# The first slot table of an attention and expert kernel, built by GpSimd instead of VectorE

## The chip, the cores and the metric

The kernel runs on one core of one Trainium2 chip. The metric is the device time of one execution in microseconds (us). Before the change, three runs took 536.79, 538.61 and 538.71 us; their median is 538.61 us. One more execution was recorded by the profiler: 537.63 us, of which its span covers 535.7 us.

The engines are named as in the profile: PE is TensorE (matmuls; PEld its weight loads), DVE is VectorE, ACT is ScalarE, POOL is GpSimd, SP is the engine that issues most transfers. An engine executes its own instructions in the order in which they stand, and waits on semaphores for the others.

## The reference, cut to what matters

Two stages follow each other: attention with rotary positions for 4 batches of 8 heads, 576 tokens and 64 features a head, and then a layer of 8 experts in which each token goes to one expert.

```
scores = scale * matmul(rotate(q), rotate(k).T);  attn = softmax(scores);  x = attn @ v     # x: [4, 576, 512]
logits = x @ w_gate                                                                      # 8 experts
for b in range(B):
    prev_e = -1
    for s in range(S):
        fresh_e = argmax(logits[b, s])
        if s == 0 or local_gate[b, s] < 0.5:  e = fresh_e
        else:                                 e = prev_e if prev_e >= 0 else fresh_e
        prev_e = e
        p = softmax(logits[b, s])
        out[b, s] = p[e] * (maximum(x[b, s] @ w1[e], 0) @ w2[e])
```

The choice of expert depends on the token before, so the tokens of an expert are known only when a batch is through attention. The kernel therefore counts them, gives each token a slot in a tile of 128 tokens of one expert, gathers the tokens of a tile by an indirect transfer, and multiplies tile by tile.

## The kernel before, in words

Attention runs over 16 pairs of heads (index p), each in 9 steps of 128 query rows, 144 steps in all (index g). A step has the score product on PE (line 273, `mm_s`), its minimum on DVE (278, `softmax_min`; the scores are negated, so the minimum is the largest score), the exponential on ACT (295), four transposes on PE (332, `tr_main`), a split of the transposed values into two parts on ACT and DVE (310 and 314, `split_to`), or in five late steps on POOL (305 and 307, `split_by_pool`), and the product with v (371, `pv_mm`), whose result ACT and DVE take out of PSUM (381 and 382).

The first three batches finish before the last one. While the last batch is in attention, their routing is computed in small parts, one a step (`route` and `early`, in the order of the string `ORDER`): logits, the largest, which token starts afresh, the expert (`experts`), and each token's rank among the tokens of its expert (`ranks`). Two results matter here. `ohr` (line 646, written by POOL in 15 comparisons of 128 x 128) holds for each block of 128 tokens a one where a token's rank modulo 128 equals the column. `tcode` (line 648) holds for each token a number made of its expert and the multiple of 128 in its rank.

The function `slots` turns these into lists of tokens. `spread_tokens` compares the codes of the n tiles with `tcode` of the tokens (line 683, a table w of 128 x (nblk x n)), and multiplies the table with the two halves of the tokens' numbers (line 687, `rhs`). `gather_tokens` multiplies `ohr` by `rhs` on PE (line 695, tile `idx`) and makes the row numbers `gidx` (700). `slots` is used twice: with first = 0, for the first six tiles from three batches (nblk = 15, n = 6), in the middle of the last batch's attention; and with first = 6, for the other 19 tiles (nblk = 20).

After the list, POOL issues the indirect transfers of the first tiles (`gather`, line 956; tile `x`). Ahead of them in its order stand the splits of the first two eighths of expert weights (`split_early`, lines 895 and 896). A tile then is transposed (`turn_x`, line 967, tile `tx`), multiplied by w1 (`first_product`, line 981, tile `h`), transposed again (1015) and multiplied by w2 (`second_product`, line 1024, tile `o`).

What sets the order: up to step 126 (g < GM) all engines follow the order of the code. From step 127 on only PE follows it (`MAN0`, later `MAN2` with DVE from the end of attention); the other engines' instructions are put in order by a scheduler when the program is built, from its own costs. The slot table falls in this last stretch, in step 140. On PE it is therefore fixed that the `idx` products (695) follow the value products of pair 14, and that the transposes `tx` of the first tile (letter x in `DRAIN`) follow all value products of pair 15 (letter u), and stand ahead of the last gate products (457) and of `h`.

Of the kernel before, what the change touches and what calls it, by code (L numbers as in the profile page):

```python
# [17 lines left out]
ALU = mybir.AluOpType  # L18
# [119 lines left out]
def tile_attention_moe(ctx, tc, qk, v, tabs, turn, consts, tri, wg, wts, out):  # L138
    nc = tc.nc
    pe, act, dve, pool, sp = nc.tensor, nc.scalar, nc.vector, nc.gpsimd, nc.sync  # L140
# [245 lines left out]
    tcode = const.tile([P, NBLK], F32, name="tcode")  # L386
# [6 lines left out]
    def bc(ap, axis, n):  # L393
        ap = ap.unsqueeze(axis)
        shape = list(ap.shape)
        shape[axis] = n
        return ap.to_broadcast(shape)
# [3 lines left out]
    def small(shape, tag, dt=F32, bufs=1):  # L401
        return sm_p.tile(shape, dt, tag=tag, name=f"{tag}_{next(ctr)}", bufs=bufs)
# [268 lines left out]
    def slots(codes, nblk, first, n):  # L671

        st = {}

        def spread_tokens():
            if first == 0:
                w, rhs = small([P, nblk * n], "c8", BF16), small([P, nblk * n * 2], "ex", BF16)
            else:
                w = et_p.tile([P, S], F32, tag="et", name="slw").bitcast(BF16)[:, 0:nblk * n]
                rhs = et_p.tile([P, S], F32, tag="et", name="slr").bitcast(BF16)[:, 0:nblk * n * 2]  # L680
            w = w.rearrange("p (j n) -> p j n", n=n)
            rhs = rhs.rearrange("p (c j n) -> p c j n", n=n, c=2)
            dve.tensor_tensor(w, bc(codes(), 1, nblk), bc(tcode[:, 0:nblk], 2, n), op=ALU.is_equal)
            yield

            tokp = C["tokp"].rearrange("p (c j) -> p c j", c=2)[:, :, 0:nblk]
            dve.tensor_tensor(rhs, bc(w, 1, 2), bc(tokp, 3, n), op=ALU.mult)
            yield
            st["rhs"] = rhs

        def gather_tokens():
            yield "pe"
            ps = ps_t.tile([P, 2, n], F32, tag="t", name=f"idx_{first}")
            for j in range(nblk):
                pe.matmul(ps, ohr[:, j], st["rhs"][:, :, j], start=(j == 0), stop=(j == nblk - 1))
            yield
            hi = small([P, n], "ihi")
            dve.tensor_scalar(hi, ps[:, 0], 64.0, None, op0=ALU.mult)
            yield
            dve.tensor_tensor(gidx[:, first:first + n], hi, ps[:, 1], op=ALU.add)  # L700
            dve.tensor_tensor(hi, hi, ps[:, 1], op=ALU.add)
            yield
            st["hi"] = hi

        def scatter_tokens():
            hi = st["hi"]
            pad = small([P, n], "ipad")
            dve.tensor_scalar(pad, hi, 0.0, BIG, op0=ALU.is_equal, op1=ALU.mult)
            yield
            dve.scalar_tensor_tensor(sidx[:, first:first + n], pad, -1.0, hi, op0=ALU.add, op1=ALU.add)  # L710
            yield

        return [spread_tokens, gather_tokens, scatter_tokens]

    def tile_experts(inc, first, n):
# [739 lines left out]
```

## Time and profile before

| engine | busy us of 535.7 | share |
|---|---|---|
| PE | 515.3 | 96% |
| DVE | 377.4 | 70% |
| POOL | 346.1 | 65% |
| ACT | 345.3 | 64% |

The profiled execution took 537.63 us, its span is 535.7 us, so 1.93 us lie around the span. An engine's busy share is a mean over stages with different limits: in attention several engines are nearly full at a time, in the expert stage PE is full and the rest have room. The chain of work that ended last runs 80% on PE and 8% on DVE. What a change is worth is read from the stage in which it stands, here from about 270 us to 292 us: the end of attention and the start of the first expert tile.

### The profile page before, as it was taken

How to read it: one execution, taken by the hardware profiler on the slowest of the kernel's cores; microseconds unless marked ns; L12 is line 12 of the kernel's file. 1: busy time of each engine (PE TensorE's matmuls, PEld its weight loads, DVE VectorE, ACT ScalarE, POOL GpSimd, SP SyncE). 2: the span in 40 equal slices, each digit the busy share in tenths (PEclk: the TensorE clock that was granted, in tenths of full speed). 3: DMA queues.
4: the chain of work that ended last, by engine and by line, in shares of the span. 5: the costliest groups of instructions: out<-in, count | busy, mean ns of one | idle time of the engine just before them, and what ended most of it. 6: DMA issues, size and time to landing. Idle time of an engine off the chain costs nothing.

```text
span 535.7 us, 10815 instructions
## 1 busy us (share of the span) xinstructions
PE 515.3 (96%) x3273; PEld 458.9 (86%) x3273; DVE 377.4 (70%) x690; ACT 345.3 (64%) x766; POOL 346.1 (65%) x290
## 2 busy tenths in 40 slices
PE   7989999999999999999999899999999999999992
PEld 4889999999999999998978688887888888888881
DVE  6999999999999999999998746446421745411540
ACT  3988999999999999998877323252533344523440
POOL 4999999999999999983898202255412554411331
PEclk9999999999999999999999999999999999999997
DMA  8658788988879878866167214653446586537440
GB/s 280 275 133 224 224 221 232 236 188 215 221 224 246 200 194 211 239 150 159 24 210 227 65 55 142 190 205 127 169 105 231 150 325 182 181 90 235 107 151 25
DMA packets 65481, 97.33 MB, mean 182 GB/s; under 512 B 28353, under 2 KB 39105, under 8 KB 65282
## 3 DMA queue, kind: packets, MB, share of 16 engines
q1 hardware_dynamic: 61938, 86.45, 57.1%
q0 software_dynamic: 3040, 9.71, 5.6%
q8 instruction: 28, 0.46, 0.4%
q14 instruction: 43, 0.35, 0.3%
q10 hardware_dynamic: 432, 0.36, 0.2%
HBM read 76.95 MB, written 12.86 MB: 168 GB/s over the span
## 4 chain that ended last, share of the span: by engine, by line
PE 80%; DVE 8%; issue 4%; ACT 3%; POOL 2%; DMA 1%; ACTq 0%; POOLq 0%; DVEq 0%
PE h L981 19%; PE o L1024 17%; PE pv L371 14%; PE s L273 13%; PE tm L332 9%; PE gx L457 3%; DVE mn L278 2%; PE th L1015 2%; DVE ptl L314 2%; PE tx L967 2%; ACT e L295 1%; PE tk L342 1%; DMA turn<-in_turn_dram 1%; ACT pth L310 1%; DVE w L926 1%
## 5 line engine op out<-in xcount | busy, mean ns | idle before, releaser
L1024 PE MATMUL o<-w,hs 128*128 128x512 f32 x456 | 113.1, 398 | 0.0
L278 DVE TENSOR_REDUCE mn<-s 128x1 f32<-128x576 f32 x144 | 107.1, 743 | 2.3 <-PE s L273 1.1
L981 PE MATMUL h<-w,xs 128*128 128x512 f32 x444 | 106.4, 393 | 1.3 <-DVE xs L314 1.0
L295 ACT ACTIVATE e<-s,mn 128x576 f32<-128x576 f32 x128 | 95.5, 746 | 15.2 <-DVE mn L278 12.6
L1030 POOL DMA_INDIRECT out_dram<-os,sidx x19 | 23.1, 1213 | 125.4 <-ACTq L932 83.7
L314 DVE TENSOR_TENSOR ptl<-tm,pth 128x512 fp32r<-128x512 f32 x139 | 95.4, 687 | 11.5 <-ACT pth L310 8.8
L273 PE MATMUL s<-m,qst 128*128 128x288 f32 x512 | 96.2, 310 | 4.1 <-ACT e L295 3.0
L981 PEld LDWEIGHTS h<-w,xs 128*128 128x128 f32 x444 | 82.5, 188 | 19.9 <-DVE w L926 1.5
L1024 PEld LDWEIGHTS o<-w,hs 128*128 128x128 f32 x456 | 83.1, 188 | 17.0 <-DVE hs L314 0.4
L310 ACT CAST pth<-tm 128x512 fp32r<-128x512 f32 x139 | 80.7, 581 | 6.8 <-PE tm L332 6.2
L273 PEld LDWEIGHTS s<-m,qst 128*128 128x128 f32 x512 | 74.1, 188 | 9.0 <-ACT e L295 5.1
L371 PE MATMUL pv<-pth,v 128*128 128x288 f32 x256 | 76.8, 315 | 0.6 <-DVE ptl L314 0.4
L332 PE MATMUL tm<-wid,e 128*128 128x128 f32 x512 | 77.1, 272 | 0.0
L371 PE MATMUL pv<-ptl,v 128*128 128x288 f32 x256 | 76.5, 314 | 0.2 <-POOL ptl L307 0.2
L200 POOL TENSOR_TENSOR stage<-stage 128x1152 f32<-128x1152 f32 x26 | 69.4, 2669 | 1.1 <-DMA stage<-in_qk_dram 1.1
L332 PEld LDWEIGHTS tm<-wid,e 128*128 128x128 f32 x512 | 62.1, 140 | 0.8 <-DVE ptl L314 0.4
L926 DVE TENSOR_TENSOR w<-stage,w 128x1024 fp32r<-128x1024 f32 x37 | 51.2, 1418 | 14.6 <-ACT w L923 9.7
L371 PEld LDWEIGHTS pv<-pth,v 128*128 128x128 f32 x256 | 48.3, 189 | 2.0 <-DVE ptl L314 0.7
L371 PEld LDWEIGHTS pv<-ptl,v 128*128 128x128 f32 x256 | 48.3, 189 | 0.5 <-POOL ptl L307 0.4
L314 DVE TENSOR_TENSOR xs<-tx,xs 128x512 fp32r<-128x512 f32 x19 | 13.1, 688 | 44.9 <-ACTq L932 35.0
L201 POOL TENSOR_TENSOR stage<-stage 128x576 f32<-128x576 f32 x26 | 37.1, 1427 | 2.0
L314 DVE TENSOR_TENSOR hs<-th,hs 128x512 fp32r<-128x512 f32 x26 | 17.4, 687 | 28.1 <-ACTq L932 16.6
(202 smaller groups left out, 821.7 us busy)
## 6 DMA issues: line engine op xcount, KB each, us to landing
stage<-in_wts_dram SPq DMA_DIRECT2D x84, 512.0 KB
stage<-in_qk_dram SPq DMA_DIRECT2D x26, 576.0 KB
qst<-xq SPq DMA_DIRECT2D x56, 128.0 KB
stage<-in_v_dram SPq DMA_DIRECT2D x16, 320.0 KB
m<-xq SPq DMA_DIRECT2D x14, 288.0 KB
m<-xk SPq DMA_DIRECT2D x14, 288.0 KB
m<-xq SPq DMA_DIRECT2D x14, 256.0 KB
m<-xk SPq DMA_DIRECT2D x14, 256.0 KB
```

What stands on the lines that cost most here:

```text
L200: engine.tensor_tensor(x, x, tab[:, 2 * f:2 * f + 2], op=ALU.mult)
L201: engine.tensor_tensor(rr[:, f], x[:, 0], x[:, 1], op=ALU.add)
L273: pe.matmul(st[:, h, lo:hi], lhs, keys[:, k0:k0 + hi - lo], start=(n == 0), stop=(n == len(parts_) - 1))
L278: dve.tensor_reduce(mn, s_t[g][:, :, 0:HALF], axis=AX.XY, op=ALU.min)
L295: act.activation(dst.rearrange("p (h s) -> p h s", h=2), s_t.pop(g)[:, :, 0:HALF], AF.Exp, bias=mn, scale=-1.0, accum_out=sums[:, col:col ...
L310: act.copy(hi, src)
L314: dve.tensor_tensor(lo, src, hi.bitcast(F32), op=ALU.subtract)
L332: pe.transpose(ps[:, k], src[:, k * P:(k + 1) * P], ident)
L371: pe.matmul(pv_t[p, u], lhs.rearrange("p c d -> p (c d)"), rhs, start=(n == 0), stop=(n == 9))
L926: (pool if k in on_pool else dve).tensor_tensor(lo, src, hi.bitcast(F32), op=ALU.subtract)
L981: pe.matmul(ps[:, c], xs_t[t][:, x, k], w[y][:, c * 512:(c + 1) * 512], start=(k == 0 and n == 0), stop=(k == 3 and n == 2))
L1024: pe.matmul(ps, hs_t[t][:, x, k], w[y][:, (k % 2) * 512:(k % 2 + 1) * 512], start=(k == 0 and n == 0), stop=(k == 7 and n == 2))
```

## The change

For the first use of `slots` (first = 0) the comparison table is written by POOL, in six instructions, one for each slot (tile) k: each compares 15 token codes a partition with one number, and writes every sixth element of w. The product with the tokens' numbers is given to POOL too. The second use (first = 6) keeps both on DVE. All lines behind line 683 move down by 4.

```diff
@@ -680,11 +680,15 @@
             w = w.rearrange("p (j n) -> p j n", n=n)
             rhs = rhs.rearrange("p (c j n) -> p c j n", n=n, c=2)
-            dve.tensor_tensor(w, bc(codes(), 1, nblk), bc(tcode[:, 0:nblk], 2, n), op=ALU.is_equal)
+            if first == 0:
+                for k in range(n):
+                    pool.tensor_scalar(w[:, :, k], tcode[:, 0:nblk], codes()[:, k:k + 1], None, op0=ALU.is_equal)
+            else:
+                dve.tensor_tensor(w, bc(codes(), 1, nblk), bc(tcode[:, 0:nblk], 2, n), op=ALU.is_equal)
             yield
 
             tokp = C["tokp"].rearrange("p (c j) -> p c j", c=2)[:, :, 0:nblk]
-            dve.tensor_tensor(rhs, bc(w, 1, 2), bc(tokp, 3, n), op=ALU.mult)
+            (pool if first == 0 else dve).tensor_tensor(rhs, bc(w, 1, 2), bc(tokp, 3, n), op=ALU.mult)
             yield
```

On POOL, before, in the last steps of attention (`ptl`, `pth`: split of transposed values; `v`: values of pair 15; `w_m`, `w_q`: the first two eighths of weights; `x`: the gathered tokens):

```order
L219 TENSOR_TENSOR v_15_4354<-stage,v_15_4354 128x10x64
L307 TENSOR_TENSOR ptl_4301<-stage,pth_4300 128x128 x3
L895 TENSOR_SCALAR w_m<-stage 128x1024
L896 TENSOR_TENSOR w_m<-stage,w_m 128x1024
L895 TENSOR_SCALAR w_q_4927<-stage 128x1024
L896 TENSOR_TENSOR w_q_4928<-stage,w_q_4927 128x1024
L956 DMA x_4938<-rows_d,gidx 128x513 x4
```

On POOL, now, at the same place (`c` is the table w, `ex` is rhs):

```order
L219 TENSOR_TENSOR v_15_4354<-stage,v_15_4354 128x10x64
L307 TENSOR_TENSOR ptl_4301<-stage,pth_4300 128x128 x3
L685 TENSOR_SCALAR c_27_4809<-tcode,code_4702 128x15 x6
L691 TENSOR_TENSOR ex_4810<-c_27_4809,cst 128x180
L899 TENSOR_SCALAR w_m<-stage 128x1024
L900 TENSOR_TENSOR w_m<-stage,w_m 128x1024
L899 TENSOR_SCALAR w_q_4932<-stage 128x1024
L900 TENSOR_TENSOR w_q_4933<-stage,w_q_4932 128x1024
L960 DMA x_4943<-rows_d,gidx 128x513 x4
```

The seven new instructions stand ahead of both weight splits and of the four gathers; nothing else on POOL has moved.

On DVE, before, in the same steps (`s`: scores; `mn`: minimum; `tm`, `tk`: transposed values; `xt`: result of a value product):

```order
L683 TENSOR_TENSOR c_27_4809<-code_4702,tcode 128x90
L278 TENSOR_REDUCE mn_4816<-s_4780 128x1
L687 TENSOR_TENSOR ex_4810<-c_27_4809,cst 128x180
L314 TENSOR_TENSOR ptl_4679<-tm_4787,pth_4678 128x4x128
L382 TENSOR_TENSOR xt_4729<-pv_1_4754,tmp_4730 64x288
L470 TENSOR_TENSOR gm_4547<-gx_0_4801,sum_3441 128x3x18
L471 TENSOR_TENSOR xrow_0_4805<-gx_0_4801,sum_3441 128x384
L278 TENSOR_REDUCE mn_4853<-s_4818 128x1
L314 TENSOR_TENSOR ptl_4679<-tm_4824,pth_4678 128x4x128
```

On DVE, now, from the same place:

```order
L278 TENSOR_REDUCE mn_4821<-s_4780 128x1
L314 TENSOR_TENSOR ptl_4679<-tm_4787,pth_4678 128x4x128
L382 TENSOR_TENSOR xt_4729<-pv_1_4754,tmp_4730 64x288
L470 TENSOR_TENSOR gm_4547<-gx_0_4801,sum_3441 128x3x18
L471 TENSOR_TENSOR xrow_0_4805<-gx_0_4801,sum_3441 128x384
L314 TENSOR_TENSOR ptl_4679<-tm_4829,pth_4678 128x4x128
L314 TENSOR_TENSOR pkl_4681<-tk_4836,pkh_4680 128x256
L470 TENSOR_TENSOR gm_4547<-gx_3_4847,sum_3441 128x2x18
L471 TENSOR_TENSOR xrow_3_4850<-gx_3_4847,sum_3441 128x256
L278 TENSOR_REDUCE mn_4858<-s_4823 128x1
```

Two instructions are gone, and the minima of the last two steps stand later among their neighbours; on ACT the exponentials of these two steps move the same way, behind one split and one copy each. The order on PE and on SP is the same as before; on PE the first `idx` product waits for POOL instead of DVE.

## Rows read from the trace of the kernel before

**Rows 1.** Chain that ended last, 255 to 330 us: start us, us, what.
```profile
272.14 1.78 DVE c L683
...
275.71 0.44 PE tk L342 x2
...
290.00 0.57 PE tx L967 x4
```

**Rows 2.** Busy time by stretch: us, PE, PEld, DVE, ACT, POOL, PE clock, DMA share, GB/s.
```profile
270.00:275.00 5.00, 4.57 (x32) 3.74 (x30) 5.00 (x8) 3.27 (x8) 4.86 (x11) 1.00 0.97 382
275.00:280.00 5.00, 4.25 (x30) 3.80 (x31) 4.94 (x12) 3.16 (x9) 4.92 (x6) 1.00 0.26 70
280.00:285.00 5.00, 4.76 (x49) 4.26 (x48) 4.07 (x15) 3.49 (x9) 4.75 (x4) 1.00 0.94 266
285.00:290.00 5.00, 5.00 (x39) 4.85 (x39) 4.42 (x9) 3.09 (x5) 4.08 (x4) 1.00 1.01 305
290.00:295.00 5.00, 5.00 (x28) 4.29 (x29) 4.40 (x10) 4.73 (x8) 4.23 (x4) 1.00 0.40 114
310.00:315.00 5.00, 5.00 (x30) 4.00 (x30) 1.38 (x7) 1.00 (x3) 0.20 (x1) 1.00 0.00 0
400.00:450.00 50.00, 50.00 (x236) 41.17 (x235) 24.08 (x23) 21.06 (x31) 20.99 (x17) 1.00 0.66 213
```

**Rows 3.** Waits of PE, 268 to 285 us: waiter, releaser, us, times, longest.
```profile
PE tk L342 <- DVE ptl L314: 0.8, 1, 0.8
```

**Rows 4.** Line 683, its two uses: ns min/median/max, first and last start, shape.
```profile
L683 DVE TENSOR_TENSOR c<-code,tcode x1: 1856/1856/1856, 272.1 to 272.1; 128x90 bf16<-128x90 f32 x1
L683 DVE TENSOR_TENSOR slw<-code,tcode x1: 553/553/553, 327.2 to 327.2; 128x380 bf16<-128x380 f32 x1
```

**Rows 5.** Timeline of POOL: start us, us, engine, line, operation, [idle before <- releaser].
```profile
273.90 0.25 POOL L767 TENSOR_SCALAR after<-take 128x8 f32<-128x8 f32 x1
274.21 0.23 POOL L768 TENSOR_SCALAR lead<-take 128x1 f32<-128x1 f32 x1
...
276.43 1.29 POOL L307 TENSOR_TENSOR ptl<-stage,pth 128x128 fp32r<-128x128 f32 x3
277.69 1.05 POOL L895 TENSOR_SCALAR w_m<-stage 128x1024 fp32r<-128x1024 f32 x1
278.82 2.40 POOL L896 TENSOR_TENSOR w_m<-stage,w_m 128x1024 fp32r<-128x1024 f32 x1
...
282.31 2.39 POOL L896 TENSOR_TENSOR w_q<-stage,w_q 128x1024 fp32r<-128x1024 f32 x1
284.88 1.28 POOL L956 DMA_INDIRECT x<-rows_d,gidx  x1 [0.17 <-DVE ipad L708]
```

**Rows 6.** Gathers issued at 284.88 and 287.78, then all 19: us to landing.
```profile
x<-rows_d,gidx POOLq DMA_INDIRECT x1, 4.9
x<-rows_d,gidx POOLq DMA_INDIRECT x1, 4.1
...
DMA to landing us min/median/max: 3.3/4.5/7.6
```

**Rows 7.** Timeline of PE and DVE around the first tile's transposes.
```profile
281.11 0.54 PE L695 MATMUL idx<-ex,ohr 128*128 128x12 bf16 x15
...
289.33 0.94 DVE L382 TENSOR_TENSOR xt<-pv,tmp 64x288 f32<-64x288 f32 x2
289.71 0.29 PE L371 MATMUL pv<-pkl,v 128*128 128x288 f32 x1
289.91 0.42 PEld L967 LDWEIGHTS tx<-wid,x 128*128 128x128 f32 x4
```

**Rows 8.** POOL's groups by line and shape: count | busy us, mean ns | idle.
```profile
L646 POOL TENSOR_SCALAR ohr<-cst,lc 128x128 bf16<-128x128 bf16 x15 | 8.8, 611 | 0.0
...
L502 POOL TENSOR_TENSOR gm<-gm 128x180 f32<-128x180 f32 x3 | 1.7, 575 | 1.1 <-DVE gm L470 1.1
...
L641 POOL TENSOR_TENSOR lc<-rk,lb 128x15 f32<-128x15 f32 x1 | 0.2, 222 | 0.0
```

## The prediction

> **What bounds the kernel now.** I read the page first: PE is busy for 96% of the span, so a change counts only through what PE waits for. Then I looked for the place: the chain of waits has line 683 on it, with 1.78 us of DVE at 272.14, and behind it a stop of PE at the transposes tk [rows 1]. The busy times by stretch show what this stage leaves to be gained. PE is busy 4.57, 4.25 and 4.76 us in the three stretches of 5 us from 270 to 285, so it idles 0.43 + 0.75 + 0.24 = 1.42 us there; from 285 to 295, and later in the expert stage, it is full [rows 2]. The largest single wait of PE is 0.8 us at tk, for a split on DVE [rows 3] that had line 683 ahead of it. Line 683 took 1856 ns for 90 elements a partition; its second use, with 380 elements, took 553 ns [rows 4]. So at least 1.3 us of the first use is not its own work but a stall on DVE.
>
> Then I read POOL, which gets the work. It is busy 4.86 and 4.92 of 5 us from 270 to 280 [rows 2], and its timeline has instruction behind instruction: the three pieces of ptl to 277.72, the weight splits from 277.69 to 282.31 + 2.39 = 284.70, and at 284.88 the first gather of tokens [rows 5]. That gather takes 4.9 us to land [rows 6], which is 284.88 + 4.9 = 289.78. PE's last value product starts at 289.71, and the weight load of tx, which reads the gathered tokens, starts at 289.91 [rows 7]: 0.13 us behind the landing. PE comes there hardly sooner than the tokens do. POOL up to the first gather is thus a second path that ends at tx, level with PE's own, and it has no slack that the trace shows.
>
> **What goes.** Two DVE instructions: 1.86 us by rows 4, and 0.55 us for line 687 (in the page's timeline of DVE at 274.51; I use it only to say that DVE is relieved). DVE's next minimum and split come earlier, the 0.8 us wait at tk goes, and PE can gain at most its whole idle time, 1.42 us, by the time it reaches tx. The minima of the last two steps, and with them two exponentials, now stand later in the order, and give some of it back. If that costs PE as much as the tk wait gave, 0.8 us, PE still arrives at tx no later than before. So PE arrives there between 0 and 1.4 us earlier; I take 0.5. What this is worth depends on the tokens.
>
> **What is added on POOL.** Six comparisons of 15 elements and a product of 180, all ahead of the weight splits and the gathers. No comparison of this size stands in the trace, so it is bounded. From below: a POOL instruction of 15 elements took 222 ns (L641) [rows 8], so six take 1.33 us. From above: the same operation with 128 elements took 611 ns (L646) [rows 8], so six take 3.67 us. The size is closer to the small rows: L767, with 8 elements, starts at 273.90, the next at 274.21 [rows 5]. I take this spacing, 0.31 us, for each: 6 x 0.31 = 1.86 us. The product has a direct row, 575 ns for 128 x 180 (L502) [rows 8]. It waits for the last comparison, for which I add 0.08 us, the gap between the end of L895 (277.69 + 1.05 = 278.74) and L896, which waits for it, at 278.82 [rows 5]. Sum: 1.86 + 0.08 + 0.58 = 2.52 us; bounds 1.33 + 0.58 = 1.9 and 3.67 + 0.08 + 0.58 = 4.3 us.
>
> The span of L767 is 0.25 us, its spacing 0.31. The Trainium skill, page "Perfetto Trace Analysis", section "GPSIMD Engine Instruction", says that GpSimd spans in a profile are unreliable and that one should time by the spacing of starts; with the span the six would be 1.5 us and the delay 0.36 us smaller. The trace agrees in so far as the two differ by 0.06 us here.
>
> **The sum.** POOL has no idle time to take this, so the first gather moves from 284.88 to 287.40. Its landing may take less time than before: 4.9 us was measured while the DMA engines were full (share 1.01 from 285 to 290, then 0.40) [rows 2]. The third gather, issued at 287.78, landed in 4.1 us; over all 19 the shortest is 3.3, the median 4.5 [rows 6]. I take 4.1, the row nearest in time, and keep 3.3 and 4.9 as ends. Landing: 287.40 + 4.1 = 291.50, against 289.78: 1.7 us later. PE, there 0.5 us earlier, waits 2.2 us for it. With both lower ends the delay is 1.9 + 3.3 - 4.9 = 0.3 us, with both upper ones 4.3 us.
>
> The Trainium skill, page "DMA: Bandwidth & Descriptors", section "Anatomy of one DMA — SWDGE (gpsimd) path", fits such a transfer by 2.0 us plus the bytes over 436e3: 128 x 513 x 4 bytes would land in 2.6 us, an estimate. By that the delay would be 2.52 + 2.6 - 4.9 = 0.2 us. No gather of the 19 was that fast, so the measured rows stand.
>
> Behind tx the delay is handed on whole. The gate products, `h` of the first tile, and what ACT and DVE do for it all follow tx in order, and from there PE is full (5.00 of 5 us at 310 to 315, 50.00 of 50 from 400 to 450) [rows 2], so nothing catches it up. What moves with POOL otherwise is covered. The `idx` products, at 281.11 before [rows 7], now need the table, which ends at 277.72 + 2.52 = 280.24; with PE up to 1.2 us earlier there the wait is at most 0.3 us, and even at the upper bound (282.0) PE reaches tx 8.8 us later (281.11 to 289.91), at 290.8, before the tokens. The row numbers come behind `idx` and were ready for POOL at 284.88; now they have 2.5 us more. The weight loads that wait for POOL's splits are for the second tile. SP's order is unchanged.
>
> In the profiled execution that is 537.63 + 1.7 = 539.3 us. The median of the runs, 538.61, lies 0.98 us above that execution, so the forecast for a median is 538.61 + 1.7 = 540.3 us.
>
> **The rivals.**
>
> First, a slower kernel: the comparison costs what the table `ohr` cost an instruction, 0.61 us, whatever its width. For it: L646 is the only row with this operation and with a number a partition to compare with. Against it: it is eight times as wide, and every other narrow POOL row is below 0.3 us. Price: 4.3 us on POOL, with a landing of 4.1 us a delay of 3.5, with 4.9 one of 4.3: 542.1 to 542.9 us. Half a per cent, 2.7 us, is what a measurement of this kernel can tell from no change; it is passed when 6 comparisons + 0.66 + 4.1 - 4.9 exceeds 2.7, from 0.47 us a comparison on.
>
> Second, the relief arrives: tx was really held by something else. For it: DVE takes the value products out of PSUM at 289.33, two in 0.94 us, so the first ended near 289.80 [rows 7], and that buffer may be what tx waited for. Against it: the landing at 289.78 is measured, so at best 0.13 us of room is left for a later one. It needs a table under 1 us, or a landing under 3 us. The gain is then what PE keeps, 0.4 to 1.4 us: 537.2 to 538.2 us.
>
> Third, the wait turns up ahead of the tokens: the later minima hold up the last exponentials, and the transposes behind `idx` wait for them. For it: both stand behind more work on DVE than before. Against it: PE has 2.2 us to give before the tokens land. It decides only above that, and would give some 541 us.
>
> **How the numbers follow.** My forecast, a delay between 0.3 and 2.7 us from the gather, gets 0.62, with a range of its own from 538.9 to 541.3 us around 540.3. The first rival gets 0.17, the second 0.15, the third 0.06. Faster by over 0.5% (under 535.9 us) would need more than PE's whole idle time in this stage; 0.03 for what I don't see. Slower by over 0.5% is the first rival and a little of the third: 0.18. The rest, 0.79, is within 0.5%. The range for 8 in 10 takes in most of the second rival and the first one's smaller prices: 537.6 to 542.6 us.
>
> **What would show it.** Right: POOL's six comparisons near 0.3 us apart and the first weight split 2.5 us later; the first gather issued near 287.4; PE idle for 1.5 to 2.5 us ahead of tx, with the gather as releaser; no wait at tk, and PE through the `idx` products somewhat earlier than 281.1. Wrong: comparisons 0.6 us apart; a gather that lands within 3 us; tx starting no later than 289.9 in the new trace, or a delay at tx that has gone by the time of the second tile.

## The result, and the profile after

The changed kernel takes 540.23 us (median of 16 runs, 538.99 to 542.16), the kernel before 537.22 us (median of 16 runs beside them, 535.68 to 538.71). The ratio is 1.0055, with a 95% interval from 1.0043 to 1.0067: slower by 2.3 to 3.6 us. That lies across the bound of 0.5%, 2.7 us, which the prediction set for "no change". The profiled execution took 540.05 us with a span of 538.1, against 537.63 and 535.7: 2.4 us longer.

**Up to the first tile's transposes.** POOL's timeline of the changed kernel comes first (start us, us, line, operation, [idle before <- releaser]; line numbers behind 683 are 4 higher than before). It answers to [rows 5].

```profile
275.88 1.30 POOL L307 TENSOR_TENSOR ptl<-stage,pth 128x128 fp32r<-128x128 f32 x3
277.16 1.91 POOL L685 TENSOR_SCALAR c<-tcode,code 128x15 bf16<-128x15 f32 x6
279.16 0.50 POOL L691 TENSOR_TENSOR ex<-c,cst 128x180 bf16<-128x180 bf16 x1
279.63 1.05 POOL L899 TENSOR_SCALAR w_m<-stage 128x1024 fp32r<-128x1024 f32 x1
...
286.84 2.07 POOL L960 DMA_INDIRECT x<-rows_d,gidx  x1 [0.17 <-DMA stage<-in_wts_dram]
```

The table stands between the start of the six comparisons, 277.16, and the first weight split, 279.63: 2.47 us. Counted from the last pieces of ptl, the first gather comes at 286.84 - 275.88 = 10.96 us; before it came at 284.88 - 276.43 = 8.45 us [rows 5]. The difference is 2.51 us, so all of the table is handed on to the gather. In absolute time the gather is 1.96 us later, because POOL's part ahead of the table already stood 0.55 us earlier.

Of these 0.55 us, 0.42 have nothing to do with the change. POOL's splits just ahead of line 683, the first place that the change touches, start at 271.65 in the profiled execution of the kernel before (line 218 behind them is used further below):

```profile
271.65 0.88 POOL L307 TENSOR_TENSOR ptl<-stage,pth 128x128 fp32r<-128x128 f32 x2
...
273.09 0.73 POOL L218 TENSOR_SCALAR v<-stage 128x640 fp32r<-128x640 f32 x1
```

In that of the changed kernel they start at 271.23:

```profile
271.23 0.86 POOL L307 TENSOR_TENSOR ptl<-stage,pth 128x128 fp32r<-128x128 f32 x2
```

The two executions differ by this head start before the change can act, so a delay that is read off their two time scales is 0.42 us too small.

The landing of this gather in the changed kernel (issue, us to landing; then all 19), which answers to [rows 6]:

```profile
x<-rows_d,gidx POOLq DMA_INDIRECT x1, 4.4
...
DMA to landing us min/median/max: 3.4/4.3/7.7
```

It lands at 286.84 + 4.4 = 291.24, 1.46 us later than before. What PE waited for from 255 to 540 us (waiter <- releaser: us, times, longest), against [rows 3], then PE's timeline around tx, against [rows 7], and tx of the kernel before:

```profile
PE tx L971 <- DMA x<-rows_d,gidx: 3.2, 1, 3.2
PE h L985 <- DVE xs L314: 1.0, 1, 1.0
PE h L985 <- ACT xs L310: 0.8, 1, 0.8
...
PE idx L699 <- POOL ex L691: 0.4, 1, 0.4
```

```profile
287.90 0.29 PE L371 MATMUL pv<-pkl,v 128*128 128x288 f32 x1
291.40 0.63 PE L971 MATMUL tx<-wid,x 128*128 128x128 f32 x4 [3.21 <-DMA x<-rows_d,gidx]
```

```profile
289.94 0.63 PE L967 MATMUL tx<-wid,x 128*128 128x128 f32 x4
```

The wait at tk is gone, the last value product starts 1.81 us earlier (287.90 for 289.71), and PE then stands for 3.21 us in front of the tokens. The relief of DVE did come through, and it was all given back at tx, whose products start at 291.40 instead of 289.94: 1.46 us later, or 1.88 us with the head start of 0.42.

The busy times of the changed kernel by stretch show the same (us, PE, PEld, DVE, ACT, POOL, PE clock, DMA share, GB/s), against [rows 2]:

```profile
280.00:285.00 5.00, 5.00 (x48) 4.77 (x45) 4.58 (x14) 3.70 (x10) 4.83 (x4) 1.00 1.05 308
285.00:290.00 5.00, 3.19 (x24) 2.95 (x23) 4.91 (x8) 2.22 (x5) 4.52 (x3) 1.00 0.46 155
290.00:295.00 5.00, 3.60 (x23) 3.27 (x24) 2.56 (x8) 2.88 (x6) 4.27 (x5) 1.00 0.75 186
...
300.00:305.00 5.00, 3.06 (x15) 1.76 (x16) 4.57 (x11) 1.69 (x4) 0.63 (x1) 1.00 0.21 65
```

PE is full from 280 to 285, where it idled before, and has the holes of 1.81 and 1.40 us behind it. The granted clock stays at 1.00 in these stretches. The last row shows a second hole, which the prediction did not have: 1.94 us from 300 to 305. The kernel before has one there too, a smaller one:

```profile
300.00:305.00 5.00, 4.00 (x19) 2.80 (x19) 4.28 (x7) 0.40 (x1) 0.00 (x0) 1.00 0.04 17
```

**Behind tx.** The place is the weight splits on DVE, line 926 before and 930 after, and what follows them in DVE's order up to the split `xs` of the second tile. First the timeline of the kernel before, with POOL's own split of one part:

```profile
291.52 2.41 POOL L926 TENSOR_TENSOR w<-stage,w 128x1024 fp32r<-128x1024 f32 x1
...
293.17 4.11 DVE L926 TENSOR_TENSOR w<-stage,w 128x1024 fp32r<-128x1024 f32 x3
297.21 0.79 DVE L507 TENSOR_REDUCE lg_all<-gm 128x45 f32<-128x360 f32 x1
...
301.12 0.68 DVE L314 TENSOR_TENSOR xs<-tx,xs 128x512 fp32r<-128x512 f32 x1
301.86 0.73 PE L981 MATMUL h<-w,xs 128*128 128x512 f32 x2 [1.00 <-DVE xs L314]
```

Then the same in the changed kernel:

```profile
294.00 2.41 POOL L930 TENSOR_TENSOR w<-stage,w 128x1024 fp32r<-128x1024 f32 x1
...
294.63 5.13 DVE L930 TENSOR_TENSOR w<-stage,w 128x1024 fp32r<-128x1024 f32 x3
299.69 0.80 DVE L507 TENSOR_REDUCE lg_all<-gm 128x45 f32<-128x360 f32 x1
...
303.67 0.68 DVE L314 TENSOR_TENSOR xs<-tx,xs 128x512 fp32r<-128x512 f32 x1
304.40 0.73 PE L985 MATMUL h<-w,xs 128*128 128x512 f32 x2 [1.00 <-DVE xs L314]
```

DVE starts its three splits 1.46 us later, which is the delay of tx, and takes 5.13 us instead of 4.11 for them, 1.02 more. Line 507 behind them is 2.48 us later, `xs` of the second tile 2.55, and PE, which waits 1.00 us for `xs` in both kernels, 2.54. Between tx and the second tile it is DVE that sets the time, not PE: from the first split to `xs` it has no stop of over 0.1 us in either trace. The other 0.8 us that PE waits in the changed kernel, for ACT's part of the same `xs`, come from there too: ACT's exponential ahead of that part (line 532) waits 1.19 us for DVE's line 529, which stands behind line 507.

Why the splits took longer is seen in their single durations. First those of the kernel before, then those of the changed one (ns min/median/max, first and last start):

```profile
L926 DVE TENSOR_TENSOR w<-stage,w x3: 1211/1212/1843, 293.2 to 296.1; 128x1024 fp32r<-128x1024 f32 x3
```

```profile
L930 DVE TENSOR_TENSOR w<-stage,w x3: 1212/1214/2864, 294.6 to 298.6; 128x1024 fp32r<-128x1024 f32 x3
```

One of the three is long, the first. In the changed kernel it starts at 294.63, while POOL's split of one part runs from 294.00 to 296.41, and it ends 2.86 us later, at 297.49: 1.08 us after POOL. In the kernel before POOL's split ended at 293.93, 0.76 us after DVE's start, and the first one took 1.84. The Trainium skill, page "SBUF — State Buffer", section "SBUF: two separate sides", says that a DVE operation with two inputs in SBUF and a GpSimd operation that reads SBUF lock the same pair of ports: who starts first keeps it for the whole instruction, and the other stands. The traces agree: a split that takes 1.21 us alone takes 1.08 from the end of POOL's.

**To the end.** The delay is still 2.48 us where tx of a later tile starts (442.00 before, 444.48 after). One group of output products behind it then takes 5.03 us instead of 4.38; they wait for `hs`. The last output products start at 521.17 instead of 518.04, 3.13 us later, and the last write is issued at 529.51 instead of 526.38. The span is only 2.4 us longer, so 0.7 us of that is regained between the last write and the end. Neither difference was tried by an experiment. With the head start of 0.42 us the span is 2.85 us longer, close to the 3.0 us between the medians.

### The profile page after: what moved, and what is told of

Its sections match the earlier page's. It is cut to its first block, busy times and chain, and to the rows that moved or that the text cites. A ratio compares the mean times of both kernels' runs of the same rounds, so it can differ in the third digit from the quotient of the medians.

```text
span 538.1 us, 10824 instructions
## 1 busy us (share of the span) xinstructions
PE 515.1 (96%) x3273; PEld 459.1 (85%) x3273; DVE 378.7 (70%) x688; ACT 345.4 (64%) x766; POOL 350.0 (65%) x297
## 5 line engine op out<-in xcount | busy, mean ns | idle before, releaser
L930 DVE TENSOR_TENSOR w<-stage,w 128x1024 fp32r<-128x1024 f32 x37 | 54.0, 1495 | 14.3 <-ACT w L927 9.6
```

The costliest lines, as they stand in the source:

```text
L930: (pool if k in on_pool else dve).tensor_tensor(lo, src, hi.bitcast(F32), op=ALU.subtract)
```

## The experiments

The kernel before ran beside every one of these kernels, with medians of 537.16 to 537.39 us; ratios are to it, from the runs of the same chip.

**1. The work on POOL alone.** The kernel before, with POOL doing seven comparisons of 15 and a product of 90 into a tile that nothing reads; DVE keeps the table.

```diff
             if first == 0:
+                w2 = small([P, nblk * n], "bw", BF16).rearrange("p (j n) -> p j n", n=n)
+                for k in (0, *range(n)):
+                    pool.tensor_scalar(w2[:, :, k], tcode[:, 0:nblk], codes()[:, k:k + 1], None, op0=ALU.is_equal)
+                pool.tensor_tensor(w2, w2, bc(C["tokp"][:, 0:nblk], 2, n), op=ALU.mult)
             dve.tensor_tensor(w, bc(codes(), 1, nblk), bc(tcode[:, 0:nblk], 2, n), op=ALU.is_equal)
```

> The kernel before, with the table left on VectorE, and GpSimd in addition made to do seven comparisons of 15 elements and a product of 90 into memory that nobody reads, at the place where the change puts its work. Order on all other engines as before. Theory (GpSimd's order delays the first gather, which holds tx): GpSimd's weight splits start some 2.5 us later, the first gather too, PE waits 1.5 to 3 us at tx, total +2.0 to +3.2 us over before, although VectorE is not relieved. Rival (the changed order of minima and exponentials on VectorE and ScalarE costs the time, GpSimd's load is free): no change, within 0.5 us.

Measured: 542.18 us (540.36 to 543.36), ratio 1.0086, 95% interval 1.0062 to 1.011. Its trace, POOL's timeline, PE's wait and one stretch:

```profile
277.25 2.22 POOL L686 TENSOR_SCALAR bw<-tcode,code 128x15 bf16<-128x15 f32 x7
...
287.05 2.06 POOL L961 DMA_INDIRECT x<-rows_d,gidx  x1 [0.17 <-DMA stage<-in_wts_dram]
```

```profile
PE tx L972 <- DMA x<-rows_d,gidx: 2.0, 1, 2.0
```

```profile
290.00:295.00 5.00, 3.44 (x15) 3.47 (x16) 2.02 (x6) 2.25 (x5) 4.27 (x5) 0.66 0.68 202
```

The order of DVE and ACT is as before, and the gather, the wait at tx and a slower kernel come all the same. So it is the work on POOL ahead of the gather that costs, and not the later minima. It cost more than expected; behind PE's stop the granted clock is 0.66 in the stretch, that is, PE ran at the lower of its levels for part of it. What the clock takes of the difference was not measured by itself.

**2. The comparisons on POOL, the product back on DVE.**

```diff
-            (pool if first == 0 else dve).tensor_tensor(rhs, bc(w, 1, 2), bc(tokp, 3, n), op=ALU.mult)
+            dve.tensor_tensor(rhs, bc(w, 1, 2), bc(tokp, 3, n), op=ALU.mult)
```

> The changed kernel with the product back on VectorE; GpSimd does the six comparisons alone. Theory: GpSimd carries about 1.9 us more instead of 2.5, the first gather comes 0.5 us earlier than in the changed kernel, total 0.4 to 0.6 us below the changed kernel (+2.2 to +2.8 over before). Rival (order of minima and exponentials): as the changed kernel, +3.0, or more, since VectorE has the product again.

Measured: 545.24 us (545.02 to 545.85), ratio 1.0147, interval 1.0121 to 1.0173. Far off the expectation. DVE's timeline in its trace, and two stretches:

```profile
279.46 1.13 DVE L691 TENSOR_TENSOR ex<-c,cst 128x180 bf16<-128x180 bf16 x1 [7.34 <-POOL c L685]
280.51 0.74 DVE L278 TENSOR_REDUCE mn<-s 128x1 f32<-128x576 f32 x1
```

```profile
275.00:280.00 5.00, 0.00 (x0) 0.00 (x0) 0.54 (x1) 0.00 (x0) 5.00 (x11) 0.95 0.39 123
280.00:285.00 5.00, 2.82 (x12) 2.82 (x13) 4.02 (x8) 1.68 (x4) 3.77 (x3) 0.50 0.47 173
```

The scheduler put the product ahead of a minimum in DVE's order. There it waits for POOL's comparisons, and DVE, ACT and PE wait behind it: PE does nothing from 275 to 280, and the clock is at its lower level in the next stretch. The run says nothing of the gather. It shows what the product on DVE costs in this order; an order in which the product stands behind that minimum was not tried.

**3 and 4. The first gather ahead of the second weight split**, in the changed kernel and in the kernel before. The gather of the first tile becomes a step of its own, one place earlier in POOL's order.

```diff
-ORDER = ".....fs.rRe.klx.c0pt...wg.1.Gi"
+ORDER = ".....fs.rRe.klx.c0pt...wgh1.Gi"
...
-            for t in range(4):
+            for t in range(1, 4):
...
+        def gather_first():
+            gather(0)
+            yield
```

> The changed kernel with the first gather of tokens ahead of the second weight split on GpSimd (3.5 us earlier in its order). Theory: the tokens land near 288, PE no longer waits for them more than 0.5 us, tx starts near 288.2 instead of 291.4, VectorE's relief reaches PE: total 0.5 to 2.5 us below before. If GpSimd's splits and VectorE's, which now meet otherwise, slow each other, the gain shrinks to 0. Rival (order of minima and exponentials): still +2 to +3 over before.

> The kernel before with the same move of the first gather. Theory: the tokens land near 286 to 287, but PE comes to tx no earlier than 289.8 because the table on VectorE still holds it up: tx at 289.8, total within 0.5 us of before, and 1 to 2 us above the changed kernel with the same move. Rival (the gather was the only thing that held PE, VectorE's table costs PE nothing): as fast as the changed kernel with the same move.

Measured: 541.56 us (539.65 to 543.72) for the changed kernel with it, ratio 1.0075 (1.0047 to 1.0102); 539.32 us (538.06 to 541.55) for the kernel before with it, ratio 1.0047 (1.0029 to 1.0064). The changed kernel's trace, DVE's splits and tx:

```profile
284.80 4.99 DVE L934 TENSOR_TENSOR w<-stage,w 128x1024 fp32r<-128x1024 f32 x2
...
293.23 6.80 DVE L934 TENSOR_TENSOR w<-stage,w 128x1024 fp32r<-128x1024 f32 x3
```

```profile
288.42 0.63 PE L975 MATMUL tx<-wid,x 128*128 128x128 f32 x4 [0.56 <-DMA x<-rows_d,gidx]
```

The trace of the kernel before with it, DVE and POOL:

```profile
293.41 5.70 DVE L930 TENSOR_TENSOR w<-stage,w 128x1024 fp32r<-128x1024 f32 x3
293.59 3.31 POOL L930 TENSOR_TENSOR w<-stage,w 128x1024 fp32r<-128x1024 f32 x1
```

The first half of the theory holds: with the gather early, tx starts at 288.42, 2.98 us sooner than in the changed kernel, after a wait of 0.56 us. The whole is slower even so. What POOL does later now meets DVE's splits: three of them take 6.80 and 5.70 us, and POOL's own pass 3.31 instead of 2.41. The order that frees the tokens moves the collision. The next runs take POOL's splits away instead.

**5 to 8. No part for POOL.** Part 6 of the first tile's weights is split by ACT and DVE like the others: in the changed kernel (5), in the changed kernel with the gather first (6), in the kernel before (7), and in the kernel before with the gather first (8).

```diff
-SPLITS = (((1, 2, 3, 4, 5, 7), (0, 6)),
+SPLITS = (((1, 2, 3, 4, 5, 6, 7), (0,)),
...
```

> The changed kernel; the split of weight part 6 of the first tile leaves GpSimd (first half to ScalarE, second to VectorE), so that GpSimd has no two-input work beside VectorE's splits from 292 to 300. Theory (collision: a VectorE split that meets a GpSimd tensor_tensor waits for its end; the three splits took 5.13 us instead of 4.11): each VectorE split near 1.21 us, four in 4.7 us, VectorE's chain up to the second tile 0.4 us shorter although it does one more; total 0.3 to 1.0 us below the changed kernel. Rival (only the late gather costs, collisions are hidden): no gain, or 0.5 to 1.2 us above the changed kernel from the extra split on VectorE.

> The changed kernel with the first gather ahead of the second weight split, and part 6 off GpSimd. With the first gather ahead alone, two of VectorE's splits from 293 on took 2.32 and 3.43 us. Collision theory: both fall to 1.21 us, one more is added, VectorE's chain is 2.1 us shorter and the total 1.5 to 2.5 us below the kernel with the gather move alone. Rival (collisions hidden): no change, or 0.5 to 1.2 us slower.

> The kernel before with part 6 off GpSimd. There one of the three splits took 1.84 us, the others 1.21. Collision theory: four at 1.21 take 4.7 us instead of 4.11, so 0 to 0.6 us slower than before. Rival (collisions hidden): 0.5 to 1.2 us slower from the extra split, or no change.

> The kernel before with the first gather ahead of the second weight split and part 6 off GpSimd. With the gather move alone the three splits took 1.21, 3.43 and 1.21 us. Collision theory: four at 1.21, VectorE's chain 0.9 us shorter, total 0.5 to 1.2 us below the kernel before with the gather move alone; the changed kernel with the same two edits is then level with it or up to 1.5 us faster. Rival (collisions hidden): no change against the gather move alone.

Measured, each beside the kernel without the edit; the last column is the difference of the two medians:

| kernel | us | ratio, 95% interval | without part 6 | ratio, 95% interval | difference |
|---|---|---|---|---|---|
| changed | 540.23 | 1.0055, 1.0043 to 1.0067 | 540.04 | 1.0056, 1.0041 to 1.007 | -0.2 |
| changed, gather first | 541.56 | 1.0075, 1.0047 to 1.0102 | 538.55 | 1.0027, 1.0015 to 1.004 | -3.0 |
| before | 537.23 | 1 | 537.93 | 1.0014, 0.9998 to 1.0029 | +0.7 |
| before, gather first | 539.32 | 1.0047, 1.0029 to 1.0064 | 537.63 | 1.001, 1.0001 to 1.0019 | -1.7 |

DVE's splits in the changed kernel without part 6, in the same with the gather first (with POOL's second split of weights), and in the kernel before with the gather first:

```profile
295.09 4.62 DVE L930 TENSOR_TENSOR w<-stage,w 128x1024 fp32r<-128x1024 f32 x4
```

```profile
285.51 5.01 DVE L934 TENSOR_TENSOR w<-stage,w 128x1024 fp32r<-128x1024 f32 x2
286.17 3.27 POOL L904 TENSOR_TENSOR w_q<-stage,w_q 128x1024 fp32r<-128x1024 f32 x1
...
293.96 4.62 DVE L934 TENSOR_TENSOR w<-stage,w 128x1024 fp32r<-128x1024 f32 x4
```

```profile
286.61 3.20 DVE L930 TENSOR_TENSOR w<-stage,w 128x1024 fp32r<-128x1024 f32 x2
293.26 4.62 DVE L930 TENSOR_TENSOR w<-stage,w 128x1024 fp32r<-128x1024 f32 x4
```

Without POOL beside them four splits take 4.62 us, less than three took in collision. Where the gather is first this gives 3.0 and 1.7 us, so there the collision is shown as a cost. Two results need a word. In the changed kernel itself the edit gained nothing that can be measured, where 0.3 to 1.0 us was expected; no gain is what the rival had forecast. Four splits from 295.09 end at 299.71, and three with the collision end at 299.76 (294.63 + 5.13): the four take 0.51 us less, but start 0.46 us later. In this execution PE had a granted clock of 0.67 from 290 to 295, and its ten gate products ahead of the splits took 2.64 us instead of 1.41. So the 1.02 us that the collision adds in the changed kernel are read from its trace alone; no run shows them by the time. And with both edits the changed kernel stays 0.9 us above the kernel before (538.55 and 537.63), where level or better was expected: its first pair of splits still meets POOL, 5.01 against 3.20 us.

**9 and 10. The second weight split off POOL as well**: its subtraction on DVE, in the changed kernel (9) and the kernel before (10), both without part 6.

```diff
-        pool.tensor_tensor(lo, staged(k), hi.bitcast(F32), op=ALU.subtract)
+        (dve if k else pool).tensor_tensor(lo, staged(k), hi.bitcast(F32), op=ALU.subtract)
```

> The changed kernel, with the second product half (lo) of the second early weight split on VectorE instead of GpSimd, and part 6 of the first tile's weights split by ACT and VectorE as all the others. GpSimd then does no two-input pass over weights beside VectorE's passes except the first one, 280.8 to 283.2. Theory (the later table delays the first gather, and what GpSimd does beside VectorE's two-input passes costs a second time): GpSimd is free 2.4 us sooner, so the first gather is issued near 284.4 and lands near 288.8; PE waits 0 to 1 us at tx; VectorE's four splits take about 4.7 us and the pair ahead of them, with the pass it now has more, about 3 x 1.21; time 0.6 to 1.6 us below the changed kernel with the first gather ahead and no part 6 (538.55), that is 537.0 to 538.0, level with before. Rival (the loss was only the gather, collisions cost nothing more): also near 537.5 to 538.5, but with splits on VectorE of over 2 us each. Rival (VectorE has no room for one more pass): it stands ahead of a split of transposed values that PE waits for, and PE loses 1.2 us or more there before tx: 539.5 or more.

> The kernel before with the same two edits. Theory: its first gather, ready with the row numbers at 284.9, moves little (the numbers are not ready sooner), so tx stays within 0.5 us of 289.9; VectorE has one pass of 1.21 us more ahead of the last transposes; time within 0.7 us of before with no part 6 (537.9). If VectorE has no room, PE waits for a split of transposed values there, and it is 1 us or more above it. The changed kernel with these edits comes out within 0.7 us of this one if table, gather and collisions are all that the change costs, and 1 us or more above it if something else is lost.

Measured: 542.37 us (540.73 to 543.05), ratio 1.0093 (1.0076 to 1.011), and 539.27 us (538.26 to 540.75), ratio 1.0041 (1.0025 to 1.0057). The trace of 9: DVE's order, PE's wait, and the two stretches around it:

```profile
281.23 0.16 DVE L705 TENSOR_TENSOR ihi<-ihi,idx 128x6 f32<-128x6 f32 x1
284.45 1.23 DVE L900 TENSOR_TENSOR w_q<-stage,w_q 128x1024 fp32r<-128x1024 f32 x1 [3.06 <-POOL w_q L899]
285.60 1.28 DVE L314 TENSOR_TENSOR ptl<-tm,pth 128x512 fp32r<-128x512 f32 x2
```

```profile
PE pv L371 <- DVE ptl L314: 3.8, 1, 3.8
```

```profile
280.00:285.00 5.00, 2.55 (x31) 2.17 (x30) 1.81 (x6) 2.69 (x8) 4.75 (x4) 1.00 1.05 341
285.00:290.00 5.00, 3.66 (x18) 3.67 (x19) 4.25 (x13) 1.66 (x3) 4.08 (x4) 0.73 0.61 175
```

The time of 9 is that of the rival, 539.5 us or more, but not for its reason. DVE has room: it is busy for 1.81 of 5 us from 280 to 285. Its new pass waits 3.06 us for POOL, which the new table made late, with the last splits of transposed values queued behind it, and PE waits 3.8 us for those. In 10 POOL is earlier by the table and the new pass does not wait; PE waits 0.8 us for a split behind it, and the edit costs 1.3 us over 537.93, as the rival had it there. The two differ by 3.1 us, far over the 0.7 us that table, gather and collisions alone were to leave: the edit gave PE a new wait for POOL, which only the late table makes long.

**One number over all of them.** Line 507 on DVE is the first instruction behind the first tile's splits in every one of these kernels. Its start in the profiled execution and the time, both less those of the kernel before, are in the table (297.21 us, and the median beside which the kernel ran; for 1 to 4 that is 537.16, for 5 to 8 537.23, for 9 and 10 537.39, for the changed kernel 537.22). The third column takes each execution's head start out: it counts line 507 from the start of the last of POOL's 15 comparisons of line 646, ahead of all that was changed (271.08 in the kernel before, 270.33 to 271.37 in the others).

| kernel | line 507 later, us | the same from line 646, us | time longer, us |
|---|---|---|---|
| 8: before, gather first, no part 6 | 0.6 | 1.0 | 0.4 |
| 7: before, no part 6 | 0.8 | 1.0 | 0.7 |
| 6: changed, gather first, no part 6 | 1.3 | 1.3 | 1.3 |
| 10: before, second split off POOL | 1.7 | 1.4 | 1.9 |
| 4: before, gather first | 1.8 | 2.1 | 2.2 |
| 5: changed, no part 6 | 2.4 | 3.0 | 2.8 |
| changed | 2.5 | 2.9 | 3.0 |
| 1: before, more work on POOL | 2.7 | 3.1 | 5.0 |
| 3: changed, gather first | 2.8 | 3.5 | 4.4 |
| 9: changed, second split off POOL | 4.3 | 4.5 | 5.0 |
| 2: changed, product on DVE | 7.2 | 7.3 | 8.1 |

By that column ten of eleven lie within 0.9 us of the time. The one that doesn't, 1, has a granted clock of 0.66 from 290 to 295 in its trace. But 2, 3, 5 and 9 have a fall of the clock too, so the clock alone is not shown to be the reason.

No version tried beats the kernel before; 7 and 8 come nearest.

## Why the prediction was right, and where it was not

The time, 540.3 against 540.23 us, is closer than its steps deserve. The base was 538.61, the median of the three runs shown, and over 16 runs it is 537.22; the delay was put at 1.7 and is 3.0. The two errors, 1.4 and 1.3 us, took each other away: that the number came out to 0.1 us is luck. The delay itself lies above the 0.3 to 2.7 us on which the chance of 0.62 was put.

- *The table on POOL:* 2.52 us predicted, 2.47 measured, and 2.51 at the gather. The choice of the spacing of narrow rows over the row with 128 elements was right: 277.16 to 279.16 for six is 0.33 us each. With it the first rival, 0.61 us a comparison, falls.
- *The landing:* 4.1 predicted, 4.4 measured. The 2.6 us of the Trainium skill's fit (page "DMA: Bandwidth & Descriptors", section "Anatomy of one DMA — SWDGE (gpsimd) path") were reached by no gather of the changed kernel either; the shortest of 19 took 3.4.
- *The relief of DVE:* "I take 0.5". It was 1.81 us at the last value product, 0.42 of which are the head start. So about 1.4, at the upper bound of 1.42. The later minima, from which I took most of it back, cost nothing: with them the wait at tk is gone and 280 to 285 is full. It made no difference to the time, since tx is set by the tokens; the wait was 3.2 instead of 2.2 us.
- *tx:* 1.7 us later predicted, 1.46 measured (289.94 to 291.40), 1.88 with the head start. Up to here the mechanism was the forecast's, and its rivals, a relief that arrives and a wait ahead of the tokens, fall.
- *The step that failed:* "Behind tx the delay is handed on whole. [...] from there PE is full". PE is full from 310 to 315 and from 400 to 450, as the rows said, but the rows in between were not read: from 300 to 305 PE was busy 4.00 of 5 us before, waiting for `xs`. There DVE's splits set the time, and these take 1.02 us more when POOL's own split, later by 2.48 (291.52 to 294.00), stands beside their start, which is later by 1.46. The sum is 1.46 + 1.02 = 2.48 at line 507, or 1.88 + 1.02 = 2.90 with the head start. It was there to be seen in [rows 4]: I read the 1856 ns of line 683 as a stall, and did not ask on what. Its two inputs are in SBUF, it stands at 272.06, and it ends at 273.92, 0.10 us after POOL's line 218, 273.82. The kernels of experiments 1, 4, 7, 8 and 10 keep this instruction on DVE too: in each it ends 0.10 us after the same line of POOL, while it takes 1.06 us in 1 and 1.83 to 1.85 in the others. So it stood until POOL was through, over more than one of POOL's instructions. That work put on POOL can stall DVE's other operations of this kind follows from it.
- *The rest of the 3.0 us:* 2.48 at line 507, 0.65 in one group of output products, less 0.7 at the end give the profiled 2.4, and with the head start of 0.42 the 2.85 us that stand against 3.0 between the medians. What is left is less than the interval of 2.3 to 3.6 us can tell. In 10 of the 16 the mean granted clock is 0.989 to 0.992 (median 540.3 us), in 6 it is 0.993 to 0.995 (median 539.7 us), and the profiled one has 0.994. A fall of the clock behind the wait at tx in part of the runs, as in the traces of 1 and 5, would fit these; the one trace of the changed kernel does not show it.

## What to carry to other kernels

A delay is handed on whole only as far as the engine that takes it over is full: read the busy times of every stretch behind the place, not only of the far ones, and follow the engine that sets the time there. When work goes from VectorE to GpSimd, count twice: what is queued behind it on GpSimd comes later, and where GpSimd then runs beside VectorE's operations with two inputs in SBUF, one of the two stands (here a split of 1.21 us took up to 3.43). A single instruction that takes three times its length is such a place already; find out what it waited for before moving anything near it.

## What the runs showed that was not expected

- The collision of the two engines goes both ways. In experiment 3 POOL's pass of 2.4 us took 3.27 and a DVE split of 1.21 up to 3.43, one after the other (ns min/median/max of the two splits from 284.8 on):

```profile
L934 DVE TENSOR_TENSOR w<-stage,w x2: 1636/2535/3434, 284.8 to 286.4; 128x1024 fp32r<-128x1024 f32 x2
```

- The issue of a gather on POOL took 2.07 us in the changed kernel, at 286.84, beside a DVE split, and 1.00 us for the next three; before it was 1.28 [rows 5].
- PE stood for 3.2 us ahead of tx in the profiled changed kernel and kept a granted clock of 1.00; in experiment 5, with a wait of 3.3 us at the same place, it was 0.67 from 290 to 295, between the two levels of 1.2 and 2.4 GHz as a mean. The transposes at tx then took up to 417 ns instead of about 270.
